# A fused retention and MLP kernel: one queue for the first loads, and a new order in its opening stage

## The chip, the cores and the metric

The kernel runs on one core of one Trainium2 chip. The metric is the device time of one execution in microseconds (us); the runs shown are executions of the same compiled program. A core has five engines that run their own instruction streams and wait for each other by semaphores: TensorE (PE in the profile; its weight loads are PEld), VectorE (DVE), ScalarE (ACT), GpSimd (POOL) and SyncE (SP). SyncE here only issues DMAs; ScalarE issues a few as well. Each of the two has a DMA queue of its own (q1 is SyncE's, q10 ScalarE's in the profile), and the core's 16 DMA engines serve both.

## The reference

A retention layer with a decaying state, for 4 batches, 8 heads, 768 positions and a head dimension of 64, and behind it a two-layer MLP with a leaky activation on 3072 tokens (512 to 2048 to 512), all in fp32:

```python
gamma = 1.0 - 2.0 ** (-5.0 - np.arange(H))
for t in range(S):
    state = gamma * state + einsum('bhd,bhe->bhde', k[:, :, t], v[:, :, t])
    y[:, :, t] = D ** -0.5 * einsum('bhd,bhde->bhe', q[:, :, t], state)
x = y.transpose(0, 2, 1, 3).reshape(B * S, H * D)
h = x @ w_in
out = np.maximum(0.01 * h, h) @ w_out
```

## The kernel before

**Tiling.** The sequence is cut into 6 chunks of 128 positions. Inside a chunk the recurrence becomes matmuls: scores of keys against queries, masked to the causal half, times the values; the state carries what older chunks left. The powers of the decay are put on the values (by key position) and on the results (by query position). The results of a chunk, for all four batches, are the block `x` of the MLP. Most MLP products run by a seven-product (Strassen-like) scheme, with sums and differences of blocks formed on VectorE; the very first ones, in `direct`, are plain products. From chunk 2 on, weights come back from a copy in DRAM that the kernel made of them in prepared form.

**Weights.** They arrive as 64-bit floating-point words, in 32 pieces of 512 KB. A piece is made fp32 in two halves: `next_powers` on ScalarE (lines 591, 595, 596) makes the exponents `z`, and `next_mantissas` on VectorE (603, 608, 615) the mantissas, and L615 joins the two. A `next_mantissas` also issues the load of a later piece when its buffer is free.

**Order.** Nothing is scheduled automatically: each engine runs its instructions in the order in which the program writes them. Tiles of a pool are reused in turn, and semaphores are placed for the data. A DMA holds one of eight completion semaphores in rotation, so that a load that takes a semaphore again waits for the earlier load's landing.

**The first 35 us**, which is where the change lies. Chunk 0 has no older state. For batch b:

- `load_qk(0, b)` (L121) brings queries and keys (512 KB), `load_v` (L124) the values and `load_k` (L127) the keys by position (256 KB each).
- `score(0, b)` (L193, 32 small matmuls, tile `ap`) makes scores in PSUM, and `masked(0, b)` (L213 on VectorE, tile `am`) the weights in SBUF.
- `decay_v(0, b)` multiplies the values by decay factors: on GpSimd (L163) for batches 0 and 1, on ScalarE (L167, eight instructions) for others.
- `values(0, b)` (L263, L252, tile `yp`) multiplies weights and values, and `taken(0, b, x)` (L308 on VectorE) scales the result into `x`.
- `direct(0, 0, x, ..., th)` (L695, tile `d`) makes the first dense products for one half of the batches in four steps of 8 matmul instructions each in the profile; each `next(steps)` is one step. Step 0 needs weight piece 0 and batches 0 and 1, step 1 piece 1, and so on.

The decay factors come from a small array of 8 rows (`decay`, 30 KB, tile `t` in the profile, L869), which TensorE spreads over partitions: the first table (`tables`, L916 to L920) has the factors of the values and is copied by ScalarE at L923; the second (`spread`, L928) has the factors of the results and is copied at L932. `keep_busy(n)` (L898) issues n matmuls on zeros whose results nobody reads, ten of them ahead of the first data.

The initial loads are issued in this order: on SyncE `qk` of batch 0, values of batches 0 and 1, weight pieces 0 and 1, `qk` and values of batch 2, pieces 2 and 3, batch 3, the keys, then chunk 1's; on ScalarE `qk` of batch 1, and behind it the decay rows.

Chunk 1's batches 0 and 1 follow with the state: `scored_later(0)` (score and mask of batch 0), then `score_apart(1, 1)` and `masked_apart(1, 1, j)` (L342 on VectorE, one for each half j) for batch 1, then `products_together(0)` (L228 reads of the state, L263, L278, L252) for both. The first seven-product group is `hidden` (L674, tiles `A_h` to `D_h`).

Of the kernel before, what the change touches and what calls it, by code (L numbers as in the profile page):

```python
# [22 lines left out]
def kernel(  # L23
# [14 lines left out]
    nc = tc.nc  # L38
# [20 lines left out]
    dec = const.tile([128, HP * C + NC * H + HP], FP32, name="dec")  # L59
# [60 lines left out]
    def load_qk(c, b, queue=nc.sync):  # L120
        queue.dma_start(out=heads[c, b][0], in_=qk[c, b])  # L121
# [38 lines left out]
    def decay_v(c, b, engine=nc.gpsimd):  # L160
        v = vals[c, b] if c >= JOINED else heads[c, b][1][:, 1]
        if engine is not nc.scalar:
            engine.tensor_tensor(out=v, in0=v,  # L163
                                 in1=gk[c].unsqueeze(2).to_broadcast([128, H, D]), op=ALU.mult)
        else:
            for h in range(H):
                engine.activation(v[:, h], v[:, h], AF.Identity, scale=gk[c][:, h : h + 1])  # L167
# [6 lines left out]
    def two_banks(name):  # L174
        return psum.tile([128, 2, HP, C], FP32, tag="att", bufs=2, name=name)

    def score(c, b):

        ps = two_banks(f"ap_{c}_{b}").rearrange("p j a t -> p j (a t)")[:, :, 0:NS]
        scores[c, b] = ps.rearrange("p j (m n t) -> p j m n t", n=3, t=C // 2)  # L180
        scores_to(heads[c, b][0], [scores[c, b][:, j] for j in range(2)])
# [3 lines left out]
    def scores_to(x, ps):  # L185
        for m in range(HP // 2):
            for i in range(2):
                for late in range(2):
                    for j in range(2):
                        s, a = i ^ j, 2 * m + i  # L190
                        to = (ps[j][ts(1 - s, 64), m, 1 + s] if late else
                              ps[j][ts(s, 64), m, 0 : 2 + s : 1 + s])
                        nc.tensor.matmul(to, lhsT=x[ts(j, 64), 1, a, ts(late, 64)],  # L193
                                         rhs=x[ts(j, 64), 0, a, late * 64 :],
                                         start=True, stop=True,
                                         skip_group_check=True)
# [3 lines left out]
    def new_am(c, b):  # L200
        i = turn[0]
        turn[0] = 1 - i
        return work.tile([128, 2, HP // 2, 3, C // 2], FP32, tag=f"am{i}", name=f"am_{c}_{b}")
# [35 lines left out]
    def values(c, b):  # L239
        if c == 0:  # L240
            sums_at[c, b] = apart(two_banks(f"yp_{c}_{b}"))
        last_values(c, b)
        first_values(c, b)
# [51 lines left out]
    def taken(c, b, xb):  # L295

        tokens_taken(c, b, xb)
        state_taken(c, b, for_state(sums_at[c, b]))
# [40 lines left out]
    def masked_apart(c, b, j):  # L339
        if j == 0:  # L340
            weights_of[c, b] = new_am(c, b)
        nc.vector.tensor_tensor(  # L342
            out=weights_of[c, b][:, j].rearrange("p m n t -> p m (n t)"),
            in0=scores[c, b][j].rearrange("p m n t -> p m (n t)"),
            in1=mask.rearrange("p n t -> p (n t)").unsqueeze(1)
                .to_broadcast([128, HP // 2, 3 * C // 2]), op=ALU.mult)
        if j == 1:
            scores[c, b] = weights_of.pop((c, b))
# [195 lines left out]
    def next_powers(scratch=None, between=None):  # L544
        n = done["powers"]
        done["powers"] += 1
        if n < N_PIECES and f64:
            powers(n, scratch, between)
        elif between is not None:
            between()  # L550

    def begin_mantissas(between=None):

        mantissas_begun(done["mantissas"], between)

    def end_mantissas():
        n = done["mantissas"]
        done["mantissas"] += 1
        mantissas_ended(n)
        if n != 3:  # L560
            load_piece(n + 4 if n < 3 else n + 3)
        if n == N_PIECES - 1:
            new_pair(2)
            for b in range(2):
                heads[2, b] = [work.tile([128, 2, HP, C], FP32, tag="qk", bufs=AHEAD,
                                         name=f"qk_2_{b}")]
            load_qk(2, 0)
            load_qk(2, 1)
            of_pair(2, 0, 1)
            of_pair(2, 0, 0)  # L570
        if n % 4 == 3 and n > 7:
            add_sums(n // 4)

    def next_mantissas():
        begin_mantissas()
        end_mantissas()
# [8 lines left out]
    def powers(n, scratch, between):  # L585

        top = raws[n].bitcast(U16).rearrange("p (h n four) -> p h n four", four=4, h=2)[:, :, :, 3]
        z = zs[n] = work.tile([128, 2, W // 2], I16, tag="z", bufs=3, name=f"z{n}")
        x = piece(n) if scratch is None else scratch

        nc.scalar.activation(x, top, AF.Prelu, alpha=float(BEND), scale=1.0 / 16,
                             bias=-7.5 / 16 - TOP)
        if between is not None:
            between()
        nc.scalar.activation(z, x, AF.Prelu, alpha=1.0 / BEND, bias=-float(BEND))
        nc.scalar.activation(z.bitcast(U16), z, AF.Relu, scale=128.0, bias=32768.0)
# [90 lines left out]
    def direct(c, u, x, g, th):  # L687

        banks = [ffs.tile([128, 2, N], FP32, tag="ff", bufs=4, name=f"d{r}_{c}_{th}")
                 for r in range(2)]  # L690
        for step in range(4):
            kh, k = divmod(step, 2)
            for r in range(2):
                for i in range(2):
                    nc.tensor.matmul(  # L695
                        banks[r][:, i, :], lhsT=block(2 * u, r + 2 * kh)[:, k, ts(i, 128)],
                        rhs=x[:, 2 * kh + th, k, :], start=(step == 0 and i == 0),
                        stop=(step == 3), skip_group_check=True)
                if step == 3:
                    nc.scalar.activation(g[:, 2 * r + th], banks[r], AF.Prelu, alpha=0.01)  # L700
            yield
# [160 lines left out]
    nothing = t[:, 0, 0, 0:64].bitcast(BF16)  # L862
    half = decay.shape[1] // 2
    load_qk(0, 0)
    load_qk(0, 1, nc.scalar)
    nc.vector.memset(t[:, 0, 0, 0:64], 0.0)
    nc.gpsimd.memset(rows[:, :half], 0.0)
    nc.vector.memset(rows[:, half:], 0.0)
# [27 lines left out]
    def keep_busy(n):  # L896
        for _ in range(n):
            nc.tensor.matmul(idle.rearrange("p i (two n) -> p (i two) n", two=2), lhsT=nothing,  # L898
                             rhs=nothing.unsqueeze(1).to_broadcast([128, 4, 128]),
                             start=True, stop=True, skip_group_check=True)  # L900

    tables = ffs.tile([128, 2, N], FP32, tag="ff", bufs=4, name="tables")
    spread = ffs.tile([128, 2, N], FP32, tag="ff", bufs=4, name="spread")
    n_gq = HP * C
# [5 lines left out]
    def scratch(name, n):  # L910
        return work.tile([128, 2, N], FP32, tag=name, name=f"{name}_x{n}")
# [17 lines left out]
                     stop=True, skip_group_check=True)  # L929
    values(0, 0)  # L930
    values(0, 1)
    next_powers(scratch("m5", 0), lambda: nc.scalar.copy(  # L932
        out=dec[:, 0:n_gq], in_=spread.rearrange("p i n -> p (i n)")))
    begin_mantissas(lambda: taken(0, 0, x))
    taken(0, 1, x)
    end_mantissas()
    next_powers(scratch("u2", 1))
    score(0, 2)
    keep_busy(1)
    steps = direct(0, 0, x, parts[0][1], 0)  # L940
    next(steps)
    next_mantissas()
    decay_v(0, 2, nc.scalar)
    load(1, 2, unit_tile(LATE[0], "in12"))
# [28 lines left out]
    def products_together(b):  # L973
        for i in range(2):
            reads(1, b + i)
        for i in range(2):
            last_values(1, b + i)
            state(1, b + i)
        for i in range(2):
            first_values(1, b + i)  # L980
# [8 lines left out]
    next(steps)  # L989
    score_apart(1, 1)  # L990
    next_powers()
    next_mantissas()
    for j in range(2):
        masked_apart(1, 1, j)
    next_powers()
    products_together(0)
    next_mantissas()
# [500 lines left out]
    m1, m4, m5, u2 = (made_of[0][:, :, i] for i in range(4))  # L1498
# [279 lines left out]
```

## Time and profile before

| what | value |
|---|---|
| median of 4 runs | 630.02 us (629.98, 629.98, 630.06, 632.85) |
| profiled execution | 630.06 us, its span 628.2 us |
| TensorE busy | 621.0 us (99%), weight loads 572.1 us |
| VectorE busy | 519.8 us (83%) |
| ScalarE busy | 286.7 us (46%) |
| GpSimd busy | 146.0 us (23%) |
| DMA | 141.01 MB, mean 224 GB/s |

The span runs from the first to the last instruction of the profiled execution; the time of the execution has another 1.9 us around it. A busy TensorE is one with a matmul in its pipeline, and is not at its peak in all of that time. The timeline names each group of like instructions with its start, its duration, and in brackets how long the engine stood idle before it and what ended that.

### The profile page before, as it was taken

The page shows a single profiled execution, that of the slowest core. Times are in us where ns is not written, and L with a number is a line of the kernel's source. Part 1 is how long each engine was busy: PE and PEld are TensorE (multiplying, and loading weights), DVE is VectorE, ACT ScalarE, POOL GpSimd, SP SyncE. Part 2 cuts the span into 40 slices and gives each one's busy share as a digit, 9 for nine tenths or more (in the row PEclk, how much of TensorE's full clock was granted, in tenths as well). Part 3 has the DMA queues.
Part 4 walks back from the last instruction along what each step waited for, and adds up shares of the span by engine and source line. Part 5 has one row for each costly group of instructions (what it writes and reads, how often), then busy time and mean ns, then how long its engine had stood idle before and what let it go on. Part 6 is the DMA issues. An engine that isn't in the chain of part 4 may idle for free.

```text
span 628.2 us, 15372 instructions
## 1 busy us (share of the span) xinstructions
PE 621.0 (99%) x6411; PEld 572.1 (91%) x6411; DVE 519.8 (83%) x799; ACT 286.7 (46%) x553; POOL 146.0 (23%) x151
## 2 busy tenths in 40 slices
PE   8999999999999999999999999999999999999997
PEld 5888888888888889898999999999999999999996
DVE  5679769889989986679888968789968789989896
ACT  4876646446444114352433433534614435546541
POOL 2000000000010110104133052330250711379373
PEclk9999999999999999999999999999999999999999
DMA  8941425547782998396976997988478568688601
GB/s 327 404 147 34 133 68 202 170 133 242 249 290 76 318 368 270 96 340 189 352 227 214 280 330 245 323 279 287 149 241 301 162 222 274 207 275 280 206 2 67
DMA packets 105942, 141.01 MB, mean 224 GB/s; under 512 B 4489, under 2 KB 84233, under 8 KB 105873
## 3 DMA queue, kind: packets, MB, share of 16 engines
q1 hardware_dynamic: 105568, 139.41, 66.6%
q8 instruction: 50, 0.82, 0.5%
q10 hardware_dynamic: 304, 0.62, 0.3%
q14 instruction: 20, 0.16, 0.1%
HBM read 113.54 MB, written 26.48 MB: 223 GB/s over the span
## 4 chain that ended last, share of the span: by engine, by line
PE 91%; DMA 4%; ACT 2%; DVE 2%; issue 0%; POOL 0%; SPq 0%; DVEq 0%; POOLq 0%; ACTq 0%
PE bank L1475 27%; PE bank L1321 14%; PE bank L674 8%; PE bank L1436 8%; PE C_h L674 4%; PE B_o L674 4%; PE A_h L674 4%; PE A_o L674 4%; PE C_o L674 4%; PE B_h L674 4%; PE D_o L674 2%; PE D_h L674 2%; DMA x_words<-in_weights_dram 1%; DMA in<-in_kv_dram 1%; PE bank L453 1%; PE bank L436 1%
## 5 line engine op out<-in xcount | busy, mean ns | idle before, releaser
L619 DVE TENSOR_TENSOR made<-made,bank 128x512 f32<-128x512 f32 (+1 forms) x96 | 55.7, 616 | 33.6 <-PE bank L1475 29.9
L1475 PE MATMUL bank<-x,wb 128*128 128x128 f32 x672 | 78.1, 276 | 0.0
L1475 PEld LDWEIGHTS bank<-x,wb 128*128 128x128 f32 x672 | 77.1, 192 | 1.0
L622 DVE TENSOR_TENSOR g<-g 128x512 f32<-128x512 f32 x96 | 66.0, 708 | 4.8 <-ACT g L1517 0.5
L1475 PE MATMUL bank<-x,wa 128*128 128x128 f32 x512 | 67.7, 275 | 0.0
L1475 PEld LDWEIGHTS bank<-x,wa 128*128 128x128 f32 x512 | 62.7, 192 | 0.5 <-ACT made L1485 0.2
L1479 ACT COPY bank<-bank 128x512 f32<-128x512 f32 (+1 forms) x32 | 16.6, 517 | 92.7 <-PE bank L1475 92.5
L619 DVE TENSOR_TENSOR g<-made 128x512 f32<-128x512 f32 x64 | 51.2, 820 | 2.9
L1475 PE MATMUL bank<-t,wa 128*128 128x128 f32 x384 | 53.4, 275 | 0.0
L1321 PE MATMUL bank<-g,w 128*128 128x128 f32 x392 | 50.5, 276 | 0.0
L1475 PEld LDWEIGHTS bank<-t,wa 128*128 128x128 f32 x384 | 48.0, 192 | 0.0
L1321 PEld LDWEIGHTS bank<-g,w 128*128 128x128 f32 x392 | 46.8, 192 | 0.1
L1517 ACT ACTIVATE g<-g 128x512 f32<-128x512 f32 x64 | 37.8, 633 | 7.2 <-DVE g L619 7.2
L674 PE MATMUL bank<-g,w 128*128 128x256 f32 x168 | 38.0, 382 | 0.0
L1436 PE MATMUL bank<-g,w 128*128 128x256 f32 x168 | 37.8, 382 | 0.0
L1291 POOL TENSOR_TENSOR x<-g 128x512 f32<-128x512 f32 x12 | 17.0, 1420 | 88.8 <-DVE t L622 20.5
L1436 PEld LDWEIGHTS bank<-g,w 128*128 128x128 f32 x168 | 31.4, 190 | 4.2
L674 PEld LDWEIGHTS bank<-g,w 128*128 128x128 f32 x168 | 31.3, 190 | 4.2
L163 POOL TENSOR_TENSOR in<-in,dec 128x512 f32<-128x512 f32 x2 | 2.5, 1268 | 139.5 <-DVE last L608 139.5
L619 DVE TENSOR_TENSOR o<-o,bank 128x512 f32<-128x512 f32 (+2 forms) x44 | 26.4, 632 | 10.0 <-ACT bank L788 4.2
L417 POOL MEMSET between<- 128x1 f32 x16 | 1.9, 117 | 132.1 <-PE bank L453 103.9
L619 DVE TENSOR_TENSOR o<-o,w 128x2048 f32<-128x2048 f32 (+2 forms) x16 | 27.2, 1717 | 0.2
(281 smaller groups left out, 1350.9 us busy)
## 6 DMA issues: line engine op xcount, KB each, us to landing
wa<-kept SPq DMA_DIRECT2D x16, 1344.0 KB, 9.1
w<-leaf_kept SPq DMA_DIRECT2D x44, 448.0 KB, 5.6
raw<-in_weights_dram SPq DMA_DIRECT2D x31, 512.0 KB, 4.3
wb<-kept SPq DMA_DIRECT2D x16, 896.0 KB, 6.5
wa<-kept SPq DMA_DIRECT2D x16, 448.0 KB, 4.3
wb<-kept SPq DMA_DIRECT2D x16, 448.0 KB, 7.3
out_dram<-o SPq DMA_DIRECT2D x23, 256.0 KB, 3.0
kept<-w SPq DMA_DIRECT2D x12, 448.0 KB, 5.6
```

The lines of the kernel that those rows point to most:

```text
L163: engine.tensor_tensor(out=v, in0=v, in1=gk[c].unsqueeze(2).to_broadcast([128, H, D]), op=ALU.mult)
L436: mm = nc.tensor.matmul(at[n][j][ts(i, 64), m, ts(h, 64)], lhsT=by_half[h][ts(j, 64), n, a], rhs=x[ts(j, 64), 0, a, ts(h, 64)], start=(n = ...
L453: mm = nc.tensor.matmul(at[n][j][ts(i, 64), m, ts(h, 64)], lhsT=val[ts(h, 64), 2 * a + j], rhs=weights[j][ts(h, 64), n, m, i], start=(n == ...
L619: return nc.vector.tensor_tensor(out=out, in0=a, in1=b, op=ALU.add)
L622: return nc.vector.tensor_tensor(out=out, in0=a, in1=b, op=ALU.subtract)
L674: nc.tensor.matmul(to, lhsT=block(w, sa)[:, k, ts(i, 128)], rhs=rhs[:, k, a:z], start=(first and (i == 0 or split) and n == 0 and k == 0), ...
L1291: op = nc.gpsimd.tensor_tensor(out=out, in0=a, in1=b, op=ALU.subtract)
L1321: nc.tensor.matmul(ps[q][:, to], lhsT=weights[i][j], rhs=moving[i][s], start=(i == 0 and m in ("M1", "M5", "M4")), stop=True, skip_group_c ...
L1436: nc.tensor.matmul(room[x][:, i, :], lhsT=block(2 * u + 1, sa)[:, k, ts(i, 128)], rhs=rhs[:, k, :], start=(first and i == 0 and k == 0), s ...
L1475: nc.tensor.matmul(ps[q][:, i], lhsT=w[:, j, i], rhs=part_of(moving[i], s), start=(i == 0 and m in ("M1", "M5", "M4")), stop=True, skip_gr ...
L1479: nc.scalar.copy(out=ps[3], in_=ps[0])
L1517: nc.scalar.activation(g[:, i], g[:, i], AF.Prelu, alpha=0.01)
```

## The change

Four edits. The load of batch 1's queries and keys goes to SyncE's queue, right behind batch 0's, and leaves the decay rows alone in ScalarE's. ScalarE's copy of the second table goes ahead of the first of piece 0's three exponent instructions, where it stood behind that one. `score(0, 2)` goes from ahead of `keep_busy(1)` and the first dense step to behind that step. In chunk 1, `next_mantissas()` (piece 4) goes behind the two masks of batch 1. No instruction is added or removed. The diff, with more of the lines around the second and third part:

```diff
     load_qk(0, 0)
-    load_qk(0, 1, nc.scalar)
+    load_qk(0, 1)
     nc.vector.memset(t[:, 0, 0, 0:64], 0.0)
     nc.gpsimd.memset(rows[:, :half], 0.0)
     nc.vector.memset(rows[:, half:], 0.0)
     nc.scalar.dma_start(out=rows[0:H], in_=decay)
     load_v(0, 0)
...
     nc.scalar.copy(out=dec[:, n_gq:], in_=tables[:, 0, 0 : n_gk + HP])
     decay_v(0, 0)
     score(0, 1)
     decay_v(0, 1)
     masked(0, 1)
     nc.tensor.matmul(spread.rearrange("p i n -> p (i n)"), lhsT=place, rhs=g_q, start=True,
                      stop=True, skip_group_check=True)
     values(0, 0)
     values(0, 1)
-    next_powers(scratch("m5", 0), lambda: nc.scalar.copy(
-        out=dec[:, 0:n_gq], in_=spread.rearrange("p i n -> p (i n)")))
+    nc.scalar.copy(out=dec[:, 0:n_gq], in_=spread.rearrange("p i n -> p (i n)"))
+    next_powers(scratch("m5", 0))
     begin_mantissas(lambda: taken(0, 0, x))
     taken(0, 1, x)
     end_mantissas()
     next_powers(scratch("u2", 1))
-    score(0, 2)
     keep_busy(1)
     steps = direct(0, 0, x, parts[0][1], 0)
     next(steps)
+    score(0, 2)
     next_mantissas()
     decay_v(0, 2, nc.scalar)
     load(1, 2, unit_tile(LATE[0], "in12"))
     masked(0, 2)
     next_powers()
     next_powers()
     next(steps)
     values(0, 2)
...
     scored_later(0)
     decay_v(1, 1, nc.scalar)
     next(steps)
     score_apart(1, 1)
     next_powers()
-    next_mantissas()
     for j in range(2):
         masked_apart(1, 1, j)
+    next_mantissas()
     next_powers()
     products_together(0)
     next_mantissas()
```

`load_qk(c, b, queue=nc.sync)` issues one DMA on the queue that it is given.

## The prediction

> **What bounds the kernel now.** I read the page first: its chain of work that ended last says which engine's time is the kernel's time.
>
> ```profile
> PE 91%; DMA 4%; ACT 2%; DVE 2%; issue 0%; POOL 0%; SPq 0%; DVEq 0%; POOLq 0%; ACTq 0%
> ```
>
> TensorE (PE) is the bound, and the edits all lie in the first 36 us, where the other shares come from. From the trace's TensorE rows I summed the idle time behind 36 us: 0.32 us in all, the longest piece 0.18 us at 256.26. So a change counts for what it does to the moment at which TensorE, from about 35 us on, runs without a break: 1 us earlier there is 1 us off the end. Next I read the timeline of the first 20 us (start, duration, engine, line, operation; in brackets the idle time before it and what ended it).
>
> ```profile
> 5.80 0.90 PE L193 MATMUL ap<-qk 64*64 64x128 f32 x32 [1.10 <-DMA qk<-in_qk_dram]
> 6.98 0.37 PE L916 MATMUL tables<-t 128*128 128x16 f32 x2 [0.28 <-DMA t<-decay_dram]
> 7.82 0.20 ACT L923 COPY dec<-tables 128x52 f32<-128x52 f32 x1 [4.38 <-PE tables L920]
> 8.16 2.04 POOL L163 TENSOR_TENSOR kv<-kv,dec 128x512 f32<-128x512 f32 x2 [5.73 <-ACT dec L923]
> 9.34 0.69 ACT L591 ACTIVATE m_x<-raw 128x512 f32<-128x512 uint16 x1 [1.32 <-DMA raw<-in_weights_dram]
> 9.56 0.92 DVE L603 TENSOR_SCALAR w<-raw 128x512 uint32<-128x512 uint32 x1
> 9.60 0.69 PE L263 MATMUL yp<-am,kv 128*64 128x64 f32 x16
> 9.93 0.58 ACT L932 COPY dec<-spread 128x512 f32<-128x512 f32 x1
> 11.42 0.68 DVE L608 SCALAR_TENSOR_TENSOR w<-raw,w 128x512 f32<-128x512 uint32 x1
> 12.01 0.90 PE L193 MATMUL ap<-in 64*64 64x128 f32 x32 [0.33 <-DMA in<-in_qk_dram]
> 12.62 0.68 DVE L615 SCALAR_TENSOR_TENSOR w<-w,z 128x512 f32<-128x512 f32 x1
> 13.35 3.86 PE L695 MATMUL d<-x,w 128*128 128x256 f32 x16
> ```
>
> This is a relay. The queries and keys of batch 0 land (5.76), batch 0's scores, the first table, its copy on ScalarE, the two decays on GpSimd (1.04 each), the values on TensorE, then VectorE's last product of weight piece 0 (L615, ends 13.30), and only then the first dense step (13.35). Batch 2's scores at 12.01 lie in time in which TensorE would wait for L615 anyway. Then the DMA rate by stretch (last two columns: busy share of the DMA engines, GB/s).
>
> ```profile
> 2.00:3.00 1.00, 1.00 (x4) 0.34 (x3) 0.00 (x0) 0.84 (x1) 0.36 (x2) 1.00 0.51 147
> 3.00:4.00 1.00, 1.00 (x4) 0.40 (x3) 0.00 (x0) 0.44 (x1) 0.00 (x0) 1.00 1.00 410
> 4.00:5.00 1.00, 0.70 (x4) 0.10 (x1) 0.00 (x0) 0.00 (x0) 0.00 (x0) 1.00 1.03 410
> ```
>
> The engines are full from 3 us on, shared by the two queues' first loads. Last, TensorE's own timeline near 33 us.
>
> ```profile
> 31.92 0.69 PE L263 MATMUL yp<-am,in 128*64 128x64 f32 x16
> 32.44 0.64 PE L278 MATMUL yp<-in 128*64 128x64 f32 x16
> 33.28 0.99 PE L263 MATMUL yp<-am,in 128*64 128x64 f32 x16 [0.20 <-issue]
> 34.10 0.64 PE L278 MATMUL yp<-in 128*64 128x64 f32 x16
> ```
>
> Undisturbed, such a group of 16 takes 0.47 to the next (for chunk 1's other two batches, groups start at 42.40, 42.87 and 43.34). Here 32.44 to 33.28 is 0.84 and 33.28 to 34.10 is 0.82: 0.37 + 0.35 = 0.72 us lost. The chain of waits names the cause: VectorE's masks of batch 1 (L342, 32.63 to 33.66) stand behind L615, which waits for ScalarE until 32.00.
>
> **Part 1, the queue.** Nothing is added; batch 1's load (0.5 MB) goes from ScalarE's queue to SyncE's, second in order. Issue costs SyncE 0.45 us, so all loads behind are issued 0.45 later. That is covered: the first values load was issued at 1.25 and landed at 7.05, queued behind bytes, not behind its issue. Without the cover it would cost 0.45. Landing of batch 0: both loads, 1.05 MB, are through at 37 + 147 + 410 + 410 KB at 5.0 us plus 0.1, and landed at 5.76 and 5.99, so 0.64 to 0.87 behind their last bytes. Alone in front, 0.52 MB is through at 3.0 + (524 - 184) / 410 = 3.83 us, landed 4.5 to 4.7. If one queue gave no more than half the rate, it would stay 5.76; I take 4.7, since one queue alone moved 414 GB/s between 8 and 9 us. The keep-busy matmuls end at 4.70 to 4.75, so scores start at 4.75, 1.05 earlier. The decay rows, alone in their queue, no longer follow 0.5 MB, and the 0.28 wait for them goes. Batch 1's data lands near 5.9 as before, and is wanted at 6.3.
>
> The relay then: scores 4.75, tables 5.6 to 6.35 (0.83 for scores, 0.72 for tables), ACT copy to 6.65, and here another wait becomes last: GpSimd needs batch 0's values, landed at 7.05. It starts at 7.15 (8.16 before): decays end 8.2 and 9.2. Batch 1's scores 6.35, the second table 7.2 to 8.3, values 8.6 and 9.6 (9.60 and 10.60 before). Gain here 1.0.
>
> A page of the Trainium skill speaks against this part: "DMA: Bandwidth & Descriptors", section "Issuing engines are not separate DMA queues", says that two issuing engines share the same DMA engines and save only issue time. By that rule alone the move loses 0.45 us and wins nothing; the 410 GB/s rows agree on sharing, but sharing is what makes batch 0 late, so order is what is won. (The instruction order of the built kernel has batch 1's scores ahead of the second table already before; that is no part of the sum.)
>
> **Part 2, ScalarE's copy of the second table** goes ahead of piece 0's exponents. Spread is ready at 8.3, piece 0 lands at 9.32: the copy (0.58) lies in that hole, and ScalarE, without a break from 9.34 to 21.2, is 0.45 to 0.5 earlier until then. VectorE: L603 at 9.36 in 0.42 (0.92 before, beside GpSimd's decay; 0.42 elsewhere), first take 9.8, then L608 at 10.4 instead of 11.42, and L615 ends 1.88 behind it: 12.3. Piece 0's landing, 9.32, is what is late next. The first dense step starts at 12.33 instead of 13.35.
>
> **Part 3, batch 2's scores** (32 matmuls, 0.83 us; no DMA) move out of the wait and behind that step. They now stand on the path: step 12.33 to 14.2, scores to 15.0, second step 15.0 instead of 15.21. Piece 1 is ready at about 14.1 and hidden. Batch 2's mask on VectorE starts at 15.1 (15.08 before), with piece 2 queued behind it; that piece waits for ScalarE till about 16.4 anyway, then is ready at 18.35, and TensorE reaches it at 18.6 (18.82). Net of parts 1 to 3: 1.02 - 0.83 = 0.2 us. Bounds: 0.8 us lost if nothing lands earlier; 0.5 won if piece 0 too comes earlier. From 18.6 to 32.7 TensorE had no wait over 0.1 us and keeps the 0.2; batch 1's keys (in 23.33) are used behind slack.
>
> **Part 4, masks ahead of piece 4.** The separate scores end near 30.8, masks 30.95 to 32.0; TensorE wants them at 32.7. The 0.72 goes. Queued behind on VectorE: pieces 4 and 5 (1.87 each) now follow the masks without a break: 32.0, 33.85, 35.7, so the takes of batches 0 and 1 start at 35.7 (35.41 before) and end at 37.3. The next user, A_h, would start at 38.71 - 0.94 = 37.77: 0.45 of cover. Without it, the part loses up to 0.25 of its gain. Piece 4's room, and load 7 with it, is free 1.2 us later; that load was in at 36.41 and first read at 41.44.
>
> Sum: 630.06 (this execution; span 628.2 and 1.9 around it; the median of the runs is 630.02) - 0.22 - 0.72 = 629.1.
>
> **Rivals.** (B) The front gains nothing: the first load is not earlier alone, or piece 0 binds. Then part 3 costs 0.8 and part 4 returns 0.72: 630.1. For it: SyncE's queue started slowly (37 GB/s in its first microsecond). Against: the wait rows for `qk` and `t`. (C) The other side: the clock. TensorE now stands still from 11.2 to 12.33 in front of the dense step, where batch 2's scores were. If that hole cools it, dense steps run at half speed. Price: at the start the weight loads of the keep-busy matmuls were 0.42 to 0.43 apart until 3.59, so about 2.7 us slow; half of that, 1.35, on the path: 629.1 + 1.35 = 630.5. It decides from a hole longer than the kernel has stood; the wait 4.70 to 5.80, as long, left the speed up, so it is unlikely.
> The Trainium skill, "TensorE: Matmul & The Clock Gate", section "Part 1: The HAM clock gate", puts the fall at an idle window of about 3.4 us; by it the hole is free, and a fall would cost an estimated 1.7 us, ending at 630.8. No row here shows a fall.
> (D) The masks' gain is given back, because VectorE, 95% busy from 50 to 60 us, becomes late: 630.06 - 0.22 = 629.8.
>
> **How the numbers follow.** Forecast 0.62 (629.1, its own range 628.8 to 629.5), B 0.13, C 0.07, D 0.13; 0.05 for what no row shows. The range 628.6 to 630.4 takes in the forecast, B, D and the 0.3 of extra gain, and leaves out C and the rest. What a measurement of this kernel can tell from no change is about 0.5%, 3.15 us. All four cases lie within it; the rest I split 0.02 faster, 0.03 slower (one run of before stood at 632.85).
>
> **What would show it.** Right: first scores at 4.7 to 4.9, POOL L163 at 7.1 to 7.3, first L695 near 12.3, scores of `in` behind its first 8, no gap before the second L263 near 32.7, A_h about 0.9 earlier. Wrong: first scores above 5.5, L695 at 13 or later, its weight loads twice as far apart, or new idle time on TensorE behind 36 us.

## The result and the profile after

The change made the kernel slower by a little: 631.21 us (median of 42 runs, 630.61 to 633.54), against 630.38 us for the kernel before (66 runs, 629.60 to 633.85). The ratio is 1.0012, 95% interval 1.0007 to 1.0018, so about 0.8 us. The forecast was 0.9 us faster than the profiled execution of before; the measured time lies outside the range, on the other side of it. By the 0.5% bound it is no change that one measurement could tell.

The profiled execution of after took 631.79 us (span 629.7). TensorE's share of the chain on the page, 91% before, is 94%: it still ends last.

```profile
PE 94%; DMA 3%; DVE 1%; issue 1%; ACT 0%; POOL 0%; DVEq 0%; POOLq 0%; SPq 0%
```

The timeline of the first 16 us answers to the one shown of before (start, duration, engine, line, operation; in brackets the idle time before and what ended it).

```profile
5.04 0.90 PE L193 MATMUL ap<-qk 64*64 64x128 f32 x32
6.77 0.37 PE L916 MATMUL tables<-t 128*128 128x16 f32 x2 [0.83 <-DMA t<-decay_dram]
7.61 0.20 ACT L923 COPY dec<-tables 128x52 f32<-128x52 f32 x1 [4.10 <-PE tables L920]
7.95 2.04 POOL L163 TENSOR_TENSOR kv<-kv,dec 128x512 f32<-128x512 f32 x2 [5.52 <-ACT dec L923]
9.39 0.69 PE L263 MATMUL yp<-am,kv 128*64 128x64 f32 x16
9.50 0.59 ACT L932 COPY dec<-spread 128x512 f32<-128x512 f32 x1 [1.69 <-PE spread L928]
9.98 0.68 ACT L591 ACTIVATE m_x<-raw 128x512 f32<-128x512 uint16 x1
12.41 0.68 DVE L615 SCALAR_TENSOR_TENSOR w<-w,z 128x512 f32<-128x512 f32 x1
13.15 1.99 PE L695 MATMUL d<-x,w 128*128 128x256 f32 x8 [1.35 <-DVE w L615]
15.07 0.90 PE L193 MATMUL ap<-in 64*64 64x128 f32 x32
15.90 1.99 PE L695 MATMUL d<-x,w 128*128 128x256 f32 x8
```

Batch 0's scores start 0.76 us earlier than before. Then the second line takes most of that away: the wait for the decay rows has not gone, it has grown from 0.28 to 0.83 us. From there every step of the relay is 0.20 to 0.21 earlier, no more, down to the first dense step (13.15; it was 13.35). Behind that step stand batch 2's scores, and the second dense step starts at 15.90. Before, its weights were loaded from 15.21 on:

```profile
15.21 1.59 PEld L695 LDWEIGHTS d<-x,w 128*128 128x128 f32 x8 [0.27 <-DVE w L615]
```

The chain of waits of after names the decay rows in one line. Its first columns are start and length of the piece:

```profile
1.59 5.05 DMA t<-decay_dram
```

The second place is TensorE and VectorE from 31 to 40 us. Before:

```profile
35.41 0.68 DVE L308 TENSOR_TENSOR x<-yp,dec 128x512 f32<-128x512 f32 x1
36.02 0.41 DVE L314 TENSOR_TENSOR states<-states,yp 128x256 f32<-128x256 f32 x1
36.95 0.41 DVE L314 TENSOR_TENSOR states<-states,yp 128x256 f32<-128x256 f32 x1
37.21 0.90 PE L193 MATMUL ap<-in 64*64 64x128 f32 x32
37.93 0.85 PE L193 MATMUL ap<-qk 64*64 64x128 f32 x32
38.71 1.99 PE L674 MATMUL A_h<-x,w 128*128 128x256 f32 x8
```

After:

```profile
31.86 1.02 DVE L342 TENSOR_TENSOR am<-ap,mask 128x384 f32<-128x384 f32 x2 [1.78 <-PE ap L193]
33.58 0.64 PE L263 MATMUL yp<-am,in 128*64 128x64 f32 x16
34.04 0.64 PE L278 MATMUL yp<-in 128*64 128x64 f32 x16
35.90 0.69 DVE L615 SCALAR_TENSOR_TENSOR w<-w,z 128x512 f32<-128x512 f32 x1
36.51 0.69 DVE L308 TENSOR_TENSOR x<-yp,dec 128x512 f32<-128x512 f32 x1
37.11 0.41 DVE L314 TENSOR_TENSOR states<-states,yp 128x256 f32<-128x256 f32 x1
37.63 0.90 PE L193 MATMUL ap<-in 64*64 64x128 f32 x32 [0.40 <-issue]
38.04 0.41 DVE L314 TENSOR_TENSOR states<-states,yp 128x256 f32<-128x256 f32 x1
38.56 0.90 PE L193 MATMUL ap<-qk 64*64 64x128 f32 x32
39.39 1.99 PE L674 MATMUL A_h<-x,w 128*128 128x256 f32 x8
```

The masks now come first, and the groups at 33.58 and 34.04 follow each other without the 0.72 us that before lost there: at 34.6 TensorE is 0.05 ahead of before, having been 0.67 late at 31. But the takes start at 36.51 instead of 35.41. Each is a scaling into `x` (L308) and a state update (L314) that read the same PSUM tile `yp`. The scores of chunk 1's next two batches start 0.11 us behind the end of the first and of the second update (37.52 to 37.63, 38.45 to 38.56); TensorE stands idle for 0.40 us ahead of the first, and the second starts 0.2 later than it would behind the first without a wait. A_h starts at 39.39; it was 38.71. The account of this execution up to there: front 0.20 won, batch 2's scores 0.83 to 0.89 lost, 0.72 won, 0.73 lost; in sum +0.68. From A_h on, the shift to before stays 0.67 to 0.68 up to 249 us.

The profiled execution itself is 1.73 longer. Of the rest, 0.67 is one wait that before's execution did not have, and 0.3 is lost between 500 us and the last matmul, to which p1 below comes back:

```profile
250.72 0.94 PE L1475 MATMUL bank<-t,wa 128*128 128x128 f32 x6 [0.67 <-DMA wa<-kept]
```

The 0.68 and the 0.3 together are 0.98; the median's 0.8, with its interval of 0.4 to 1.1, is about that. Late landings came and went between profiled executions (none over 0.3 us after 40 us in those of before and of the third and fourth part alone, two in that of after_t below); the comparison of the parts therefore goes by TensorE's position at A_h and by the medians, not by the ends of single executions.

### The profile page after: what moved, and what is told of

Read it like the earlier page. It is cut to its first block, busy times and chain, and to the rows that moved or that the text cites. A ratio compares the mean times of both kernels' runs of the same rounds, so it can differ in the third digit from the quotient of the medians.

```text
span 629.7 us, 15372 instructions
## 1 busy us (share of the span) xinstructions
PE 621.4 (99%) x6411; PEld 572.2 (91%) x6411; DVE 520.1 (83%) x799; ACT 286.5 (45%) x553; POOL 145.4 (23%) x151
## 4 chain that ended last, share of the span: by engine, by line
PE 94%; DMA 3%; DVE 1%; issue 1%; ACT 0%; POOL 0%; DVEq 0%; POOLq 0%; SPq 0%
PE bank L1475 26%; PE bank L1321 14%; PE bank L1436 8%; PE bank L674 8%; PE C_h L674 4%; PE B_o L674 4%; PE A_h L674 4%; PE C_o L674 4%; PE A_o L674 4%; PE B_h L674 4%; PE d L695 2%; PE D_h L674 2%; PE D_o L674 2%; DMA wa<-kept 1%; PE bank L453 1%; PE bank L436 1%
## 5 line engine op out<-in xcount | busy, mean ns | idle before, releaser
L163 POOL TENSOR_TENSOR in<-in,dec 128x512 f32<-128x512 f32 x2 | 2.5, 1266 | 139.5 <-DVE last L608 139.5
```

## The experiments

After the result there were two theories on where the expected 0.9 us had gone, and they needed each part by itself. Theory 1: the parts add, the decay rows hold part 1, and part 4 gives its gain back at 37 us through the room of the scores. Theory 2: part 3 and part 4 hang together (the shift of 0.8 us in the front changes which wait is there at 33 us), so that neither price holds alone. "A_h" below is its start against 38.71 in before. The kernel before was run beside each group of experiments, at 630.43 us (p1, p3, p4, p4t), 630.39 (p123, after_t, rows, best) and 630.46 (p1s, p2, r8). Each profile is one execution, and the front differs between executions by some tenths.

**p1: the queue alone.** Edit:

```diff
-    load_qk(0, 1, nc.scalar)
+    load_qk(0, 1)
```

> Part 1 alone (batch 1's first load on SyncE's queue). Issue-order theory: the decay rows are served behind the 1 MB issued before them whichever queue holds them, so the first table starts near 6.7 us and the first dense step near 13.15; pieces land 0.1 to 0.3 later; total -0.2 to +0.3 against before. Rival (the prediction's): rows alone in a queue land by 4.5 us, table near 5.6, first dense step near 12.3.

Measured: 631.19 us, ratio 1.0010 (1.0002 to 1.0019). The tables' matmul starts at 6.54, the first dense step at 13.18, A_h at 38.61: the front wins 0.1 to 0.2, not 1.0, as in after. The rows landed at 6.38. But the median is worse by 0.76, which A_h does not explain. Two things further on do. In the profiled execution the time from the last matmul's end to the end of the span is 4.14 us instead of 3.55. The last lines of the two timelines, of before and then of p1:

```profile
622.72 1.92 PE L674 MATMUL bank<-g,last_s 128*128 128x256 f32 x12
624.74 0.91 SPq L801 DMA_DIRECT2D out_dram<-o  x2
625.08 0.37 ACTq L801 DMA_DIRECT2D out_dram<-o  x1
```
```profile
623.03 1.92 PE L674 MATMUL bank<-g,last_s 128*128 128x256 f32 x12
625.05 0.90 SPq L801 DMA_DIRECT2D out_dram<-o  x2
625.67 0.39 ACTq L801 DMA_DIRECT2D out_dram<-o  x1
```

ScalarE issues its last output 0.34 us behind SyncE's first in before, and 0.62 behind it in p1. p1's trace has an 8 KB transfer of instructions at 626.9, which in before lies at 611.3.

The other is on TensorE: between 500 us and its last matmul it loses 0.3 us, in two steps near 524 and 611 us. The same 0.28 to 0.32 is in all eight kernels here in which the issue of the first loads is changed (after, p1, p123, after_t, rows, best, p1s, r8), and 0.01 at most in p2, p3, p4 and p4t. What causes it is open. With 0.10 won at A_h, 0.3 and 0.6 of the tail make p1's 0.8.

**p3: batch 2's scores alone** behind the first dense step.

```diff
-    score(0, 2)
     keep_busy(1)
     steps = direct(0, 0, x, parts[0][1], 0)
     next(steps)
+    score(0, 2)
```

> Part 3 alone (batch 2's scores behind the first dense step). Interplay theory: second dense step near 16.0 instead of 15.21, TensorE 0.7 to 0.8 late up to 32 us, but the 0.72 us of waiting for batch 1's masks near 33 us shrinks to nothing, since those masks follow ScalarE and not TensorE: total 0.0 to +0.2. Rival (parts add up as priced): +0.8.

Measured: 631.26 us, ratio 1.0011 (1.0003 to 1.0020). The second dense step is at 16.27, A_h 1.02 late, and the mask wait is still there, at 34.3, with the usual 0.7. So the move costs about the 0.83 that its 32 matmuls take, which is also what the median says; some 0.2 more is of this execution, whose decay rows landed 0.16 later (7.00) and whose first dense step came 0.17 later (13.52). It does not touch the wait of part 4: theory 2 falls.

**p4: the masks alone** ahead of piece 4, as in the change's last hunk.

```diff
     next_powers()
-    next_mantissas()
     for j in range(2):
         masked_apart(1, 1, j)
+    next_mantissas()
```

> Part 4 alone (masks ahead of piece 4). Give-back theory: no wait near 33 us, but pieces 4 and 5 then stand between the masks and the takes of chunk 1's batches 0 and 1, the scores of batches 2 and 3 need the PSUM room that the takes free, and wait near 37 us: A_h at 38.6 to 38.8, total -0.1 to +0.1. Rival (as priced): -0.72, A_h near 38.0.

Measured: 630.25 us, ratio 0.9996 (0.9988 to 1.0005): nothing that can be told. Its timeline shows why:

```profile
33.33 0.64 PE L278 MATMUL yp<-in 128*64 128x64 f32 x16
36.40 0.41 DVE L314 TENSOR_TENSOR states<-states,yp 128x256 f32<-128x256 f32 x1
36.91 0.90 PE L193 MATMUL ap<-in 64*64 64x128 f32 x32 [0.40 <-issue]
37.32 0.41 DVE L314 TENSOR_TENSOR states<-states,yp 128x256 f32<-128x256 f32 x1
37.84 0.90 PE L193 MATMUL ap<-qk 64*64 64x128 f32 x32
38.66 1.13 PE L674 MATMUL A_h<-x,w 128*128 128x256 f32 x4
```

At 33.33 TensorE is 0.77 ahead of before (34.10 there), at A_h only 0.05. Again each group of scores starts 0.1 us behind the end of a state update (36.81, 37.73). In the code both come from one pool of two PSUM buffers (L175, tag `att`): a score needs the buffer that the last reader of `yp` leaves. That is where the gain is given back.

**p4t: p4, and piece 5 behind the takes,** which takes the suspected cause away.

```diff
     products_together(0)
-    next_mantissas()
...
     taken(1, 1, x1)
+    next_mantissas()
```

> Part 4, and piece 5's mantissas behind the takes of chunk 1's batches 0 and 1 (everything else as before the change). Give-back theory: no wait near 33 us and none near 37 us, A_h near 38.0, total -0.6 to -0.75. Rival (VectorE is full from here on and returns it elsewhere whatever the order): -0.2 to +0.2.

Measured: 629.59 us, ratio 0.9986 (0.9975 to 0.9996): faster than before, by 0.8 us. (One run of 1650 us is left out.) The timeline:

```profile
34.30 0.69 DVE L308 TENSOR_TENSOR x<-yp,dec 128x512 f32<-128x512 f32 x1 [0.40 <-PE yp L252]
35.84 0.41 DVE L314 TENSOR_TENSOR states<-states,yp 128x256 f32<-128x256 f32 x1
36.32 0.90 PE L193 MATMUL ap<-in 64*64 64x128 f32 x32
37.82 1.99 PE L674 MATMUL A_h<-x,w 128*128 128x256 f32 x8
```

The takes start 1.5 us earlier than in p4, and now wait for TensorE, not the other way round. The second update is over at 36.25, ahead of the first score; the scores have no wait, and A_h is 0.89 earlier than in before, 0.17 of it from the stretch up to 31 us; the other 0.72 is the gain that was forecast for part 4. With the takes moved and nothing else, the give-back is gone: shown.

**p123: the change without part 4.**

> The change without part 4 (pieces and masks of chunk 1 in the old order). Theory that the parts add (front +0.68, masks 0.0 because the takes return their gain): A_h near 39.4, the 0.72 wait near 33 us back, total +0.6 to +0.9 against before, as the whole change. Rival (part 4's late takes are what makes the change slower): about 0 against before.

Measured: 631.71 us, ratio 1.0015 (1.0007 to 1.0024). The mask wait is back in its old place, 0.80 later than in before:

```profile
34.08 0.99 PE L263 MATMUL yp<-am,in 128*64 128x64 f32 x16 [0.21 <-issue]
```

A_h is 0.80 late. The second dense step was only 0.38 late here; the other 0.42 is from a wait of 0.55 at 24.2, ahead of the second part of batch 3's values, where before and after lose 0.1. The view names no cause for it (`issue`); ScalarE's decayed values of that batch were done at 21.2. By median the front's three parts cost 1.3, by the profile 0.8 at A_h; its tail has the 4.14 us of p1, and the 0.3 behind 500 us is there too. After's tail is 3.56, so the 0.5 us between the medians of p123 and after need be no gain of the masks: the tails alone differ by 0.6.

**after_t: the whole change, and piece 5 behind the takes** (the edit of p4t on top of it).

> The whole change, with piece 5's mantissas behind the takes of chunk 1's batches 0 and 1. Theory (parts add): 0.8 less than the change, -0.1 to -0.3 against before, A_h near 38.5. Rival (with TensorE 0.7 late the order of VectorE's work is worth nothing): as the change, +0.8.

Measured: 630.56 us, ratio 1.0003 (0.9993 to 1.0013); A_h 0.29 earlier than in before, 0.97 earlier than in after, of which 0.24 came about in the front of that execution. So about 0.65 to 0.7 comes back (the medians of after and of this differ by 0.65), and with it the change stands level with before: what parts 1 to 3 lose is what part 4, so mended, wins.

**rows: the change, with the decay rows second on SyncE's queue**, between batch 0's load and batch 1's. This takes away what part 1 was thought to wait for.

```diff
-    load_qk(0, 1)
...
-    nc.scalar.dma_start(out=rows[0:H], in_=decay)
+    nc.sync.dma_start(out=rows[0:H], in_=decay)
+    load_qk(0, 1)
```

> The whole change, but the decay rows are issued on SyncE's queue as the second load, between batch 0's and batch 1's queries and keys. Issue-order theory: the rows land by about 4.9, tables start near 5.95 right behind batch 0's scores, GpSimd near 7.15, the copy of the second table lies ahead of piece 0's landing, the first dense step starts near 12.6; total 0.4 to 0.6 less than the change. Rival (eight rows land late wherever they stand, because such a small load is slow by itself): tables near 6.7, total as the change.

Measured: 631.72 us, ratio 1.0020 (1.0008 to 1.0032). The rows landed at 5.01, 1.6 earlier than in after, which shows that their place in the order of issue was what held them. But the gain was not there:

```profile
6.58 0.40 PE L916 MATMUL tables<-t 128*128 128x16 f32 x2
7.46 0.90 PE L193 MATMUL ap<-qk 64*64 64x128 f32 x32
8.24 2.06 POOL L163 TENSOR_TENSOR kv<-kv,dec 128x512 f32<-128x512 f32 x2 [5.82 <-DMA kv<-in_kv_dram]
10.51 0.69 ACT L591 ACTIVATE m_x<-raw 128x512 f32<-128x512 uint16 x1 [0.47 <-DMA raw<-in_weights_dram]
```

In this execution the tables had no wait for data; TensorE came to them late, since batch 0's scores began at 5.43 and took 1.22 us. And the values (L163 waits for them) and piece 0 (L591 waits for it) landed about 1 us later than in after. SyncE issues the rows at 1.59 only, once they may be written, so batch 1's load behind them goes out at 2.01 instead of 1.25, and all loads behind that too. The DMA rate fell as well (as before, the last two columns; the stretch is that in which the rows landed):

```profile
4.00:5.00 1.00, 1.00 (x4) 0.29 (x2) 0.00 (x0) 0.00 (x0) 0.00 (x0) 1.00 0.87 274
```

After moved 415 GB/s in that stretch. The rate was lower at 6 to 7 us too, 152 against 262. How much of the lateness is the later issue, and how much the small load, is not shown. A_h is 1.54 late, 0.86 later than in after; 0.24 of that is there at the second dense step, and most of the rest is a wait like p123's, 0.74 at 25.0. One wait was changed for later ones.

**best: rows so placed, the copy ahead, masks ahead and piece 5 behind the takes; batch 2's scores where they were.**

> Decay rows second on SyncE's queue, the copy ahead of the exponents, batch 2's scores left ahead of the first dense step, masks ahead of piece 4 and piece 5 behind the takes. Theory: first dense step near 13.0 (batch 2's data lands near 12.1 and its scores take 0.83), second near 14.9, no wait at 33 or 37 us, total -1.0 to -1.3 against before. Rival (front is bound by the landing of pieces): second step at 15.1 to 15.2, total as the masks alone, -0.8.

Measured: 630.93 us, ratio 1.0009 (1.0000 to 1.0017): a miss. The tables are early (6.19), but both that came behind the rows are late:

```profile
7.51 0.90 PE L193 MATMUL ap<-qk 64*64 64x128 f32 x32 [0.49 <-DMA qk<-in_qk_dram]
10.47 0.69 ACT L591 ACTIVATE m_x<-raw 128x512 f32<-128x512 uint16 x1 [0.38 <-DMA raw<-in_weights_dram]
13.15 0.90 PE L193 MATMUL ap<-in 64*64 64x128 f32 x32 [1.68 <-DMA in<-in_qk_dram]
```

Batch 2's queries, in front of the first dense step again, land at 13.0, so that step starts at 14 us (13.35 in before). Part 3's place would not have mended this: in rows, which has it, the values behind the second dense step start at 18.07, here at 17.76. A_h is 0.51 late, with a wait of 0.63 at 24.7 like p123's.

**p1s: p1 and one tiny instruction more on ScalarE,** to see whether p1's tail is a matter of where its instructions are fetched.

```diff
+    one_more = const.tile([128, 1], FP32, name="one_more")
+    nc.scalar.copy(out=one_more, in_=mask[:, 0, 0:1])
```

> Part 1 alone, with one more tiny ScalarE instruction near the start (a copy of a 128 x 1 column that nobody reads). Code-loading theory: part 1 alone takes one instruction out of ScalarE's stream, which puts a load of ScalarE's code between the last matmul and the end (tail 4.14 us instead of 3.55); with the instruction back the load lies near 612 us, the tail is 3.55, and the total 0.5 to 0.7 less than part 1 alone, near 630.5. Rival (part 1's +0.8 comes from the loads, not from the tail): near 631.2, as part 1 alone.

Measured: 630.82 us, ratio 1.0003 (0.9989 to 1.0016). The tail is back at 3.55 us and the 8 KB transfer of instructions is at 612.6, so one copy moves it: the mechanism is there. The other kernels agree. Where the profile records 709 or 710 instructions of ScalarE (before, after, p3, p4, p4t, after_t, p1s, p2, r8), the last such transfer ahead of the end lies at 610 to 613 us and the tail is 3.55 to 3.58; with 708 (p1, p123) it lies at 627 to 628 and the tail is 4.14, with 707 (rows, best) at 628 to 629 and 3.76. Part 1 takes a DMA issue out of ScalarE's stream, part 4 puts a semaphore instruction in, so that the whole change is at 709 again. By median it gives 0.37 us back, less than the 0.59 of the tail, and the two intervals overlap. Its profiled execution had A_h 0.86 late, p1's 0.10 early: piece 0 landed 0.6 later in this one, by which the first dense step came at 13.74. So part 1's front varies between executions by as much as it was to win. The 0.3 behind 500 us is here too: it is a loss of part 1 beyond the tail, and 630.46 + 0.3 is near the median.

**p2: the copy alone** ahead of piece 0's exponents, as in the change's second hunk.

> Part 2 alone (ScalarE's copy of the second table ahead of piece 0's first exponent instruction). Theory: the table is ready at 9.66, after piece 0 has landed at 9.3, so the exponents start 0.6 to 0.9 later (9.34 before), piece 2 is ready later and the third dense step with it: A_h 0.1 to 0.4 later than 38.71, total 0.0 to +0.4. Rival (the prediction's: the copy is hidden and ScalarE wins half a microsecond): A_h as before or earlier, total 0.0 to -0.2.

Measured: 630.44 us, ratio 1.0003 (0.9994 to 1.0012). The copy runs at 9.80, L591 starts at 10.28 (9.34 in before), A_h is 0.35 late in this execution; by median there is nothing to be told. By their medians the four parts alone add up to 1.4 us (0.76, -0.02, 0.83 and -0.18); without p1's 0.6 of tail, which the whole change does not have, that is 0.8, as measured. This is what theory 1 says, within the noise of four medians.

**r8: p4t, part 2, and the decay rows as ScalarE's first load.** The tables' matmuls read 8 partitions instead of 128, so that the rows need no zeros around them and can be issued at once.

```diff
     load_qk(0, 0)
-    load_qk(0, 1, nc.scalar)
-    nc.gpsimd.memset(rows[:, :half], 0.0)
-    nc.vector.memset(rows[:, half:], 0.0)
     nc.scalar.dma_start(out=rows[0:H], in_=decay)
+    load_qk(0, 1, nc.scalar)
...
-        rows[:, i:j] for i, j in zip(ends, ends[1:]))
+        rows[0:H, i:j] for i, j in zip(ends, ends[1:]))
```

> Masks ahead of piece 4 with piece 5 behind the takes, the copy ahead of the exponents, and the decay rows as ScalarE's first load: the tables' matmuls read the 8 rows alone, so that no zeros have to be written first, and the rows are issued at 0.8 us; batch 1's queries and keys follow on ScalarE's queue. Issue-order theory: rows land before 5, batch 0 by 4.8, first scores at 4.7 to 5.5, GpSimd at 7.1 to 7.3, first dense step 12.5 to 13.0, total 0.3 to 0.6 less than p4t, 1.1 to 1.4 less than before. Rival (the landing of pieces, not the relay, sets the second dense step): total as p4t, -0.8.

Measured: 629.49 us, ratio 0.9988 (0.9979 to 0.9997). The rows landed at 2.95, batch 0 at 4.75, batch 1 at 6.83:

```profile
4.89 0.90 PE L193 MATMUL ap<-qk 64*64 64x128 f32 x32
5.72 0.39 PE L914 MATMUL tables<-t 8*128 8x16 f32 x2
6.93 2.04 POOL L163 TENSOR_TENSOR kv<-kv,dec 128x512 f32<-128x512 f32 x2 [5.02 <-ACT dec L921]
12.79 2.54 PE L695 MATMUL d<-x,w 128*128 128x256 f32 x11
```

This is the relay that the prediction drew, 1.2 us ahead of before at L163. At the first dense step 0.56 of it is left, since batch 2's queries land at 11.6 and their scores again stand in front. A_h is at 37.37, 1.34 earlier than in before; 0.29 of it is lost again behind 500 us, as in p1, and the profiled execution is the fastest of this kernel's 11 runs. The median is only 0.1 below p4t's; the two can't be told apart, and both beat before.

## Why the prediction was wrong, step by step

**The scale.** The forecast stood on an execution of 630.06 us; the median of before over 66 runs is 630.38. So 0.3 of the 2.1 us between forecast and result is the scale. The rest is the expected 0.9 that did not come, and a loss of 0.8.

**What bounds the kernel: right.** TensorE runs without a break from A_h on, and what is late there is late at the end, but for late landings that differ between executions (0.67 us at 250 us in after's) and the 0.3 us behind 500 us, which no sum of the prediction had.

**Part 1: the queue. One term failed, and with it most of the gain.** Batch 0 alone in front lands at 4.46 (4.5 to 4.7 forecast). The failed step is "The decay rows, alone in their queue, no longer follow 0.5 MB, and the 0.28 wait for them goes." They were issued at 1.59 on a queue with nothing else in it, and their first packets moved at 4.90 us, when 0.94 of the 1.05 MB of both batches was through on the other queue; they landed at 6.63 (6.84 before). The prediction read an empty queue as a free road. It held the rows to follow only what stood ahead in their own queue, where the runs show that they follow what was issued earlier on either: 2.95 when issued first (r8), 4.84 to 5.01 second (rows, best), 6.3 to 6.7 third (after, p1, p123, after_t, p1s). So the tables start at 6.77 where 5.6 was forecast, and L163 at 7.95 where 7.15 was, 0.20 gained instead of 1.0. Part of that is a second, smaller miss: scores were set at 4.75, by the end of the keep-busy matmuls in one execution; in after's it was 5.04, and in other executions these matmuls ended as late as 5.50, since the full clock came later.

The Trainium skill, "DMA: Bandwidth & Descriptors", section "Issuing engines are not separate DMA queues", was weighed against the trace and set aside. It says that DMAs of different issuing engines run on the same 16 DMA engines and interleave there, and that a second issuing engine saves only issue time. The rates go with it: 410 GB/s from 3 to 5 us with two queues before, 410 and 415 with one after. So do the 5.76 and 5.99 of before, where two loads issued together shared. That loads issued one after the other interleave is not what after and r8 show: there the second engine gave a small load no earlier turn. The 0.45 us of issue that by this page alone the move loses did not show: the first values landed at 7.04, before at 7.05.

**Part 2: the copy. Wrong as it stands.** It needed the second table to be ready at 8.3 and piece 0 at 9.32. The first came at 9.46, for want of part 1's gain, and piece 0 landed at 9.50; the copy (9.50 to 10.09) then stands in front of the exponents instead of in a hole, and L591 starts at 9.98, 0.64 later than before. That is hidden until 12.4, where VectorE's L615 comes 0.21 earlier than before all the same. In r8, where the table is early, the copy runs at 8.86 and L591 at 9.35, as in before.

**Part 3: right in its price.** 0.83 on the path; the second dense step is 0.69 late with 0.20 gained ahead of it, and p3 alone is 1.02 late at A_h. The bound "0.8 us lost if nothing lands earlier" is what happened.

**Part 4: the gain right, what is late next wrong.** The 0.72 at 33 us went, as forecast. The failed step is "The next user, A_h, would start at 38.71 - 0.94 = 37.77: 0.45 of cover." A_h is not the next user of what VectorE's takes release. The scores of chunk 1's batches 2 and 3 stand ahead of it on TensorE and need the PSUM buffers that the takes read. The sum had the takes "end at 37.3", 1.6 after their start: that is the end of the second scaling, which A_h reads. The state update behind it reads the same buffer, and with it the takes last 1.95 (35.41 to 37.36 before). With pieces 4 and 5 ahead of the takes, the buffers come free at 37.52 and 38.45, and TensorE wanted the first at 37.23, so the cover was below nothing: the loss at 37 us is 0.73, not "up to 0.25". p4 shows it without the other parts, p4t takes it away.

**The rivals.** B, the front gains nothing and part 3 costs 0.8 (630.1), was nearest, but kept part 4's 0.72. D, the masks' gain given back, was right as to the outcome and wrong as to place: it comes at 37 us through PSUM room, not at 50 to 60 us through VectorE's load. What came true is B and D together: nothing in front to pay for part 3's 0.83, and the masks' gain given back, 630.06 + 0.83 = 630.9 on before's scale, or 630.7 with the 0.20 that the front did win (the measured 0.8 puts it at 630.9); they were given chances as if only one of them could hold. C, the clock, did not happen: TensorE stood still 1.35 us ahead of 13.15, and the eight weight loads behind it took 1.59 us as in before; the granted clock on record stays at full.

## What to carry to other kernels

Before a stall on the bounding engine is counted as won, list the next uses of every buffer, PSUM too, that the delayed instructions would have released: the first waiter is the next in the engine's order, not the next one that reads the delayed result. A small load that a chain starts with belonged, here, first in the order of issue over all queues, not alone in another queue. And where several rivals could hold at once, price them together.

## What the runs showed of the hardware

- The first loads were served in the order of their issue over both queues, not side by side. In after, the decay rows, issued 0.8 us later than batch 0 on an empty queue, moved only when the other queue was nearly through with what was issued before them. In r8 SyncE's queue moved 0.05 MB between 5 and 6 us, when batch 0's queries, keys and values were through, and ScalarE's 0.33 MB of batch 1, issued at 1.42 us; SyncE's next load, issued at 1.72, came behind it (landings 6.83 and 7.70). In before, two loads issued at the same time (0.80) did share, and landed at 5.76 and 5.99.
- Of the first microseconds from 3 to 9, the rate was lowest from 6 to 7 us in every kernel here (248 GB/s in before, 262 in after, 283 in r8, 152 in rows). The 30 KB load into 8 partitions is not shown to be the cause: in r8 it had landed at 2.95. In rows, where it landed at 5.01, the rate was low at 4 to 5 us too (274).
- The trace's record of the granted clock is at full from 3.75 us (before) to 6.59 us (p2) after the start, by execution. The keep-busy matmuls follow each other by 0.40 to 0.43 us until then and by 0.21 to 0.22 behind it (in before from 3.89 to 4.32); ten of them therefore ended between 4.7 and 5.5 us.
- A change of one or two instructions on ScalarE moved an 8 KB instruction transfer from 612 us to 627 us, into the last output's way, and the tail from 3.55 to 4.14 us (p1, p123, p1s).
- TensorE lost 0.3 us behind 500 us in every kernel that changed the issue of the first loads, 0.01 at most in those that did not; the cause is open.
